# Four equal weight slices, a new order of the first products, one K^T V block and a later place for half of the transposes, in a fused linear-attention and ELU-MLP kernel

## The chip, the cores and the metric

The kernel runs on one core of one Trainium2 chip. Times are device microseconds of that core. "TensorE" (PE) multiplies matrices, PEld is its weight load, "DVE" is VectorE, "ACT" ScalarE, "Pool" GpSimd. PSUM is the memory into which TensorE writes; this kernel divides it into eight banks. The recorded texts call the transposes "turns". A ratio is the mean time of one kernel's runs over that of the other's of the same rounds, so it is not quite the ratio of the medians quoted.

## The reference, cut to what matters

```python
kv  = einsum('bhsd,bhse->bhde', k, v)          # per batch and head: K^T V, 64 x 64
out = einsum('bhsd,bhde->bhse', q, kv)         # "se" below
x   = out / sqrt(mean(out^2) + 1e-6) * g_norm  # RMS norm over each head, 64 wide
h   = x @ w_in                                 # 4608 x 512 @ 512 x 2048
y   = elu(h) @ w_out                           # 4608 x 2048 @ 2048 x 512
```

There are 8 batches, 8 heads and 576 rows a batch. The kernel treats 512 rows of each batch as one group and the 64-row rests of all batches as a ninth.

## The kernel before: the parts that the change touches

The load of `w_in` in five uneven slices (a slice holds columns, and product `f` of the MLP needs columns 128 f to 128 f + 127 over all four chunks `c` of 128 rows). Pool issues these loads; they turn float32 into bfloat16 on the way.

```python
edges = (0, 512, 768, 1280, 1664, 2048)
for lo, hi in zip(edges, edges[1:]):
    load_w_in(slice(lo, hi))
```

Batch 0. `x0[:, c]` is the normalised input's chunk c. It comes out of a chain through TensorE, ACT and DVE, one chunk after the other. `first(fs, cs)` emits the products of those f for those c, c outermost; product f is complete after c = 3.

```python
products = {0: pair[:, 0, :], 1: pair[:, 1, :], 2: bank(6), 3: bank(7), 4: bank(0)}
first((0, 1, 2, 3), (0,))
mean0[3] = bank(2)
mean_first(3); log_first(3); exp_first(3); scale_first(3)      # makes x0[3]
first((0, 1, 2, 3), (1,))
first((4,), (0, 1))
first((0, 1, 2, 3, 4), (2,))
products[5] = bank(1)
first((5,), (0, 1, 2))
first((0, 1, 2, 3, 4, 5), (3,))
# ... then ELU of the pair (0, 1), of (2, 3), of (4, 5)
for i in range(3, 8):                                         # mm1(0, i): products 2i, 2i+1
    mm1(0, i, relu=i in (3, 5, 7), home={5: "m2", 6: "at"}.get(i, "m1"))()
```

`mm1(0, 4)` writes the two banks that the pair had, so it must wait until DVE has read the pair.

Batch 1's attention is woven into batch 0's second matrix product `mm2`:

```python
at["kv0"]()                       # K^T V, half of the heads, with its eviction by ACT
for j in order[:3]:
    mm2(0, j, 8, 10)
at["kv1"]()                       # the other half
mm2(0, order[3], 8, 10)
at["se"](...)
# ... norm, mul0, mul1 (DVE), more mm2, then:
        if j == 0:
            at["x0"]()            # transposes of rows half 0 by TensorE; ACT: PSUM -> xT
at["x1"]()                        # the same for half 1; DVE: PSUM -> xT
# ...
for cs in (slice(0, 256), slice(256, G)):     # batch 1's first products, by column halves
    for f in range(4):
        for c in range(KC):
            nc.tensor.matmul(firsts[f // 2][:, f % 2, cs], lhsT=w_in_sb[:, c, ...], rhs=xT[1](c, cs), ...)
```

`x0` and `x1` put their transposes into the two halves of one PSUM tile, `at`. The first column half needs only `x0`, the second needs `x1`.

## Time and profile before

| | before |
|---|---|
| time, median of 6 runs | 285.84 us (285.73 to 286.19) |
| span of the profiled run | 284.1 us |
| TensorE busy | 275.6 us, 97% |
| start to start of 512-column products | 216 ns (8 in 1.73 us) |

The page of the profile, its line of busy times and its chain of waits:

```profile
PE 275.6 (97%) x2131; PEld 131.0 (46%) x2162; DVE 159.2 (56%) x231; ACT 153.1 (54%) x221; POOL 54.8 (19%) x95
...
PE 88%; ACT 4%; DVE 3%; DMA 2%; issue 1%; another core or an unknown queue 1%; SPq 0%; DVEq 0%
```

TensorE is the limit. The list of waits for TensorE (who waited for whom, microseconds in total, times, longest):

```profile
PE bank L529 <- DVE zeros L506: 1.2, 1, 1.2
PE at L305 <- ACT xT L312: 0.4, 1, 0.4
PE h_ps L398 <- DVE gT L429: 0.3, 1, 0.3
PE bank L607 <- DMA w_in_sb<-in_moe_w_in_dram: 0.3, 1, 0.3
...
```

These idle times understate what is lost. A 512-column product lasts 379 ns in the trace, but the next starts after 216 ns, so a product that starts late first uses up 0.16 us of overlap before the engine counts as idle. The loss is the start-to-start time less 216 ns: an idle of 0.30 is a loss of 0.46. Three losses and two blocks stand in the timeline of TensorE (start, length, what, how many; in brackets the idle time before it and what ended it):

```profile
14.49 0.60 PE L607 MATMUL h_ps<-xT,w_in_sb 128*128 128x512 bf16 x2
...
16.91 0.61 PE L607 MATMUL bank<-xT,w_in_sb 128*128 128x512 bf16 x2 [0.30 <-DMA w_in_sb<-in_moe_w_in_dram]
...
20.37 1.89 PE L398 MATMUL h_ps<-xT,w_in_sb 128*128 128x512 bf16 x8
22.57 3.61 PE L398 MATMUL h_ps<-xT,w_in_sb 128*128 128x512 bf16 x16 [0.31 <-DVE gT L429]
...
33.02 1.08 PE L185 MATMUL at<-ident,q_pk 128*64 128x128 bf16 x32
...
37.59 0.48 PE L174 MATMUL at<-v_pk,k_pk 64*64 64x64 bf16 x36
38.00 1.25 PE L445 MATMUL o_ps<-w_out_sb,gT 128*128 128x512 bf16 x5
39.40 0.48 PE L174 MATMUL at<-v_pk,k_pk 64*64 64x64 bf16 x36
...
40.35 0.41 PE L201 MATMUL at<-kv_sb,qT 64*128 64x64 bf16 x16
...
47.30 0.61 PE L305 MATMUL at<-ident,xs 128*128 128x128 bf16 x8 [0.37 <-ACT xT L312]
47.74 2.46 PE L803 MATMUL h_ps<-xT,w_in_sb 128*128 128x256 bf16 x21
```

To be seen: product 4 waits at 16.91 for its slice of `w_in` (landed 16.86); `mm1(0,4)` waits at 22.57 for DVE to read the pair; K^T V of batch 1 (line 174) comes in two blocks, after the first transpose of q (line 185) and before "se" (line 201); and `x1`'s transposes (line 305) wait at 47.30 for ACT's `xT`, after which the products of line 803 follow at once.

### The profile page before, as it was taken

Reading aid. Unit: us, or ns where it says so; the run is one execution under the profiler, and the core shown is the slowest. Engines: PE = TensorE matmul, PEld = TensorE weight load, DVE = VectorE, ACT = ScalarE, POOL = GpSimd, SP = SyncE. Lnnn points to the kernel's source line nnn. Section 1 sums busy time; section 2 is a strip of 40 time slices with the busy share of each in tenths; the row PEclk is TensorE's granted clock in tenths of the full one; section 3 lists DMA queues with packets and bytes.
Section 4 is the critical chain, followed back from the end, with each engine's and each line's share of the span. In section 5 each row is a group of like instructions: output and inputs, shape, how many; then the busy total and the mean of one; then the engine's idle time right before and its main releaser. Section 6 shows DMA issues by size and latency. Waiting matters only on the chain.

```text
span 284.1 us, 5184 instructions
## 1 busy us (share of the span) xinstructions
PE 275.6 (97%) x2131; PEld 131.0 (46%) x2162; DVE 159.2 (56%) x231; ACT 153.1 (54%) x221; POOL 54.8 (19%) x95
## 2 busy tenths in 40 slices
PE   8999999999999999999999999999999999999994
PEld 3434545545444444444444444444444444444443
DVE  2339516598378636934684458544864486444400
ACT  2769545766496338633773378246923692333311
POOL 7834402261421061004210421012000000000000
PEclk9999999999999999999999999999999999999999
DMA  7999999796994589357934794355253123010122
GB/s 195 204 204 202 206 202 178 219 140 118 199 183 75 150 121 196 74 146 95 221 77 119 110 215 90 96 127 157 45 90 89 77 45 102 2 74 0 74 76 74
DMA packets 56507, 35.99 MB, mean 127 GB/s; under 512 B 32804, under 2 KB 54052, under 8 KB 56484
## 3 DMA queue, kind: packets, MB, share of 16 engines
q0 software_dynamic: 20736, 17.30, 40.1%
q1 hardware_dynamic: 35348, 17.83, 23.7%
q10 hardware_dynamic: 400, 0.52, 0.5%
q8 instruction: 17, 0.28, 0.4%
q14 instruction: 6, 0.05, 0.1%
HBM read 36.70 MB, written 9.44 MB: 162 GB/s over the span
## 4 chain that ended last, share of the span: by engine, by line
PE 88%; ACT 4%; DVE 3%; DMA 2%; issue 1%; another core or an unknown queue 1%; SPq 0%; DVEq 0%
PE h_ps L398 39%; PE o_ps L445 36%; PE o_ps L857 5%; DMA st_q<-in_q_dram 2%; PE at L174 2%; PE h_ps L803 1%; DVE ss L218 1%; PE at L201 1%; ACT elu_e L410 1%; ACT sq L213 1%; PE at L398 1%; PE bank L577 1%; PE bank L529 1%; ACT o_sb L458 1%
## 5 line engine op out<-in xcount | busy, mean ns | idle before, releaser
L398 PE MATMUL h_ps<-xT,w_in_sb 128*128 128x512 bf16 x524 | 123.7, 379 | 0.5 <-DVE gT L429 0.3
L445 PE MATMUL o_ps<-w_out_sb,gT 128*128 128x512 bf16 x488 | 118.1, 379 | 1.3 <-issue 0.2
L410 ACT ACTIVATE elu_e<-h_ps 128x1024 bf16<-128x1024 f32 (+1 forms) x72 | 70.9, 996 | 84.3 <-PE h_ps L398 78.9
L398 PEld LDWEIGHTS <-w_in_sb 128*128 128x128 bf16 x536 | 50.9, 98 | 62.0 <-DVE xT L333 1.7
L445 PEld LDWEIGHTS <-gT 128*128 128x128 bf16 x512 | 49.6, 98 | 58.8
L421 DVE TENSOR_SCALAR elu_e<-elu_e 128x1024 bf16<-128x1024 bf16 (+1 forms) x75 | 32.0, 426 | 73.0 <-ACT elu_e L410 73.0
L429 DVE TENSOR_TENSOR gT<-elu_e,h_ps 128x1024 bf16<-128x1024 bf16 (+1 forms) x53 | 62.6, 1181 | 5.9 <-DVE elu_e L421 0.5
L218 DVE TENSOR_REDUCE ss<-sq 128x16 f32<-128x1024 bf16 x16 | 19.3, 1218 | 13.2 <-ACT sq L213 12.3
L458 ACT COPY o_sb<-o_ps 128x512 f32<-128x512 f32 x32 | 18.5, 586 | 14.4 <-PE o_ps L445 14.4
L150 POOL COPY q_bf<-q_pk 128x512 bf16<-128x512 bf16 x24 | 14.7, 643 | 22.8 <-DMA q_pk<-in_q_dram 22.8
L416 ACT ACTIVATE elu_h<-h_ps 128x1024 bf16<-128x1024 f32 (+1 forms) x19 | 18.5, 989 | 0.0
L429 DVE TENSOR_TENSOR gT<-elu_e,elu_h 128x1024 bf16<-128x1024 bf16 x19 | 13.3, 699 | 2.5 <-ACT elu_h L416 1.2
L857 PE MATMUL o_ps<-w_out_sb,gT 128*128 128x512 bf16 (+1 forms) x79 | 14.0, 336 | 0.1
L125 POOL COPY gate<-qT 1x1 bf16<-1x1 bf16 x6 | 1.1, 180 | 63.9 <-DMA qT<-q_bf 63.9
L229 DVE TENSOR_TENSOR xs<-at,ss 128x512 bf16<-128x512 f32 x18 | 11.5, 682 | 1.2 <-ACT ss L225 1.2
L104 POOL DMA_DIRECT2D q_pk<-in_q_dram x14 | 10.7, 771 | 3.8 <-DMA w_out_sb<-in_moe_w_out_dram 1.7
L857 PEld LDWEIGHTS <-gT 128*128 128x128 bf16 x80 | 7.7, 98 | 6.4 <-DVE gT L429 0.4
L213 ACT ACTIVATE sq<-at 128x1024 bf16<-128x1024 f32 x9 | 9.4, 1044 | 1.6 <-PE at L201 1.6
L118 POOL DMA_DIRECT2D v_pk<-in_v_dram x12 | 8.6, 716 | 3.7 <-DMA w_out_sb<-in_moe_w_out_dram 2.1
L118 POOL DMA_DIRECT2D k_pk<-in_k_dram x12 | 8.3, 694 | 4.7 <-DMA w_in_sb<-in_moe_w_in_dram 3.0
L529 PE MATMUL bank<-zeros 128*128 128x512 bf16 x19 | 7.3, 508 | 1.4 <-DVE zeros L506 1.2
L865 ACT COPY o_last<-o_ps 128x512 f32<-128x512 f32 (+1 forms) x5 | 2.5, 500 | 10.8 <-PE o_ps L857 10.8
(73 smaller groups left out, 140.0 us busy)
## 6 DMA issues: line engine op xcount, KB each, us to landing
out_dram<-o_sb SPq DMA_DIRECT2D x16, 512.0 KB, 3.0
q_pk<-in_q_dram POOLq DMA_DIRECT2D x14, 256.0 KB, 4.9
k_pk<-in_k_dram POOLq DMA_DIRECT2D x6, 576.0 KB, 8.0
v_pk<-in_v_dram POOLq DMA_DIRECT2D x6, 576.0 KB, 11.2
w_out_sb<-in_moe_w_out_dram POOLq DMA_DIRECT2D x3, 512.0 KB, 14.8
st_q<-in_q_dram SPq DMA_DIRECT2D x2, 512.0 KB, 4.9
w_in_sb<-in_moe_w_in_dram POOLq DMA_DIRECT2D x2, 512.0 KB, 8.9
st_q<-in_q_dram SPq DMA_DIRECT2D x16, 64.0 KB, 2.5
```

The lines of the kernel that those rows point to most:

```text
L118: nc.gpsimd.dma_start(out=raw[name, b].rearrange("p h j d -> p h (j d)")[:, hs], in_=in_[:, hs])
L150: eng.tensor_copy(out=out_, in_=in_)
L213: nc.scalar.activation(sq, se_ps, AF.Square)
L218: nc.vector.reduce_sum(out=ss, in_=sq.rearrange("p c (h e) -> p (c h) e", h=H), axis=AX.X)
L398: nc.tensor.matmul(h_ps[a][:, cs], lhsT=w_in_sb[:, c, f * P : f * P + P], rhs=x(c, cs), start=(c == 0), stop=(c == KC - 1),)
L410: nc.scalar.activation(e[:, lo:hi, :], ps, AF.Exp)
L416: nc.scalar.activation(h[:, lo:hi, :], ps, AF.Relu)
L421: nc.vector.tensor_scalar(out=e[:, lo:hi, :], in0=e[:, lo:hi, :], scalar1=1.0, scalar2=1.0, op0=ALU.min, op1=ALU.subtract,)
L429: nc.vector.tensor_tensor(out=gT[T][:, 2 * i + lo : 2 * i + hi, :], in0=e[:, lo:hi, :], in1=h, op=ALU.add if relu else ALU.max,)
L445: nc.tensor.matmul(o_ps[T, j], lhsT=gT[T][:, f, j * P : j * P + P], rhs=w_out_sb[:, f, :], start=(f == 0), stop=(f == FC - 1),)
L458: nc.scalar.copy(o_sb[T][:, j % 2, :], o_ps.pop((T, j)))
L857: nc.tensor.matmul(ps, lhsT=gT[B][:, f, j * P : j * P + P], rhs=w_out_sb[:, f, cols], start=(f == 0), stop=(f == FC - 1),)
```

## The change

Its intent, as far as the edit shows it, is to have the first pair of products ready earlier, so that ACT and DVE start the ELU earlier, at the price of bringing products 4 and 5 later; to load `w_in` in fewer, equal pieces; to save one K^T V block; and to do something useful with the wait before `x1`, whose transposes move to a later place, behind the first half of batch 1's products over the first columns.

```diff
-    edges = (0, 512, 768, 1280, 1664, 2048)
+    edges = (0, 512, 1024, 1536, 2048)
...
-    first((0, 1, 2, 3), (1,))
-    first((4,), (0, 1))
-    first((0, 1, 2, 3, 4), (2,))
     products[5] = bank(1)
-    first((5,), (0, 1, 2))
-    first((0, 1, 2, 3, 4, 5), (3,))
+    first((0, 1, 2, 3), (1, 2))
+    for f in (0, 1, 2, 3):
+        first((f,), (3,))
+    for f in (4, 5):
+        first((f,), (0, 1, 2, 3))
...
-    at["kv0"]()
-    for j in order[:3]:
+    mm2(0, order[0], 8, 10)
+    at["kv"]()
+    for j in order[1:]:
         mm2(0, j, 8, 10)
-    at["kv1"]()
-    mm2(0, order[3], 8, 10)
...
-    at["x1"]()
...
+    head_x1 = at["x1"]
...                                   # in batch 1's first products, after f's c loop:
+            if cs.start == 0 and f == 1:
+                head_x1()
```

## The prediction

> **What bounds the kernel.** TensorE. The page of before has it busy 275.6 us of 284.1 (97%), and the chain of waits is 88% PE. The list of waits shows only about 2.9 us of PE idling named to a cause, 1.2 of it at the start. So nothing here can win much: only the stalls before 52 us can move. A 512-column product starts every 216 ns in the timeline (8 in 1.73 us), which agrees with the Trainium skill, "TensorE: Matmul & The Clock Gate", "Back-to-back issue gap" (N/2.4 + 2.5 ns, isolated). Measured by start-to-start minus 216 ns, the stalls are:
> - 16.91 us: 0.46 us, product 4 waits for the second w_in slice (landed 16.86);
> - 22.57 us: 0.47 us, mm1(0,4) waits for its banks until DVE has read the first pair (22.51);
> - two K^T V blocks in batch 1: 0.50 us each; the single block of batch 2 costs 0.80, so the split costs 0.2;
> - 47.30 us: 0.53 us, x1's turns wait for ACT's xT of x0.
>
> **The change.** PE and DVE keep the same number of instructions; ACT has one eviction fewer, Pool one load and some rows fewer.
>
> 1. Slices. DMA stays saturated to 50 us (about 205 GB/s). Packets of 512 B took 60 ns, of 768 B 79, of 1024 B 98, so equal slices save queue time: I estimate 0.25 us for all loads behind. The second slice is larger and lands about 17.0-17.9 instead of 16.86. By "DMA: Bandwidth & Descriptors", "Why a DMA increments its semaphore by 16 and not by 1", the slowest of 16 engines sets a landing; the trace agrees: a slice's packets end about 1 us before it lands.
>
> 2. Order of first products. Products 0-3 over c=2 follow at once, waiting for x0[2] (DVE ends 16.49): stall 0.1. Over c=3 they need x0[3] (17.91), and no filler is left: a new stall of 0.55 from 17.42 to 17.97. The 0.46 stall goes, as products 4 and 5 come at 18.83, after their slice. They end at about 20.56 (before 20.37), 0.2 later. But the pair is ready at 18.6 instead of 19.7, so ACT and DVE run 1.1 us ahead, DVE is done with the pair at 21.4, and mm1(0,4) starts without a stall at 22.28 instead of 22.57. Net gain 0.28.
>
> 3. One K^T V: gains 0.2. It comes at about 37.7, its second half at 38.1; the last v lands at 37.6-37.8, so a wait there is small or none. Its eviction has 1.3 us of products before se.
>
> 4. x1 inside. The first products themselves need ACT's xT, so the 0.53 stall stays and only changes its name. Then x1 comes 0.87 us later, DVE's xT (0.75 us, starting 0.33 after the last turn) ends at 49.65 on the old clock, and the second column half, ready at 49.49, waits: a loss of 0.2.
>
> All of it is on PE's chain, and after 52 us PE waits for nothing, so the sum passes through: -0.28 -0.20 +0.21 = about -0.27 us.
>
> **Predicted:** 285.5 us, 8 in 10 between 285.0 and 286.0; faster by over 2%: 0.01, within 2%: 0.98, slower by over 2%: 0.01.
>
> **What would show it.** The stall at product 4 and at mm1(0,4) gone; a new wait of about 0.55 us on DVE's xT near 18 us; first exp near 18.6; one K^T V block, se about 0.48 us earlier; a wait of about 0.5 on ACT's xT before the first batch-1 products and about 0.2 on DVE's xT before their second half. The rest shifted, equal in shape.
>
> **What would make it wrong.** The second slice landing after 18.8; v's last half landing after 38.1; x1 not waiting for xT but something I misread, so that the swap frees 0.5 us; DMA delay shifting a later wait onto PE.

## The result

| | before | after |
|---|---|---|
| time, median of 6 runs each | 285.84 us (285.73 to 286.19) | 285.62 us (285.57 to 285.80) |
| ratio, 95% interval | | 0.999 (0.9977 to 1.0003) |
| span of the profiled run | 284.1 us | 283.7 us |
| ACT instructions counted | 221 | 220 |
| Pool instructions counted | 95 | 94 |

The predicted time was 285.5 us, and the measured one lies within its range; so does the time of before, so the range alone tests little. The times alone do not separate the two kernels, since the interval contains 1. The trace does separate them, as the same anchors can be compared in both. First the page's lines, then the waits of TensorE in the kernel after:

```profile
PE 274.4 (97%) x2131; PEld 130.5 (46%) x2162; DVE 159.9 (56%) x231; ACT 153.1 (54%) x220; POOL 53.5 (19%) x94
...
PE 90%; ACT 3%; DVE 3%; DMA 2%; issue 1%; SPq 0%
```

```profile
PE bank L529 <- DVE zeros L506: 1.2, 1, 1.2
...
PE h_ps L607 <- DVE xT L598: 0.4, 1, 0.4
PE h_ps L802 <- ACT xT L312: 0.4, 1, 0.4
...
```

The waits for the slice of `w_in` and for the pair (`L398 <- DVE gT`) are gone. A wait for DVE's `xT` on line 607 is new. The wait for ACT's `xT` is as long as before, 0.4 us, and has only changed its owner: it now stands on the products (line 802) instead of on `x1`'s transposes (line 305). The timeline of TensorE after:

```profile
14.37 0.61 PE L607 MATMUL h_ps<-xT,w_in_sb 128*128 128x512 bf16 x2
...
17.85 0.59 PE L607 MATMUL h_ps<-xT,w_in_sb 128*128 128x512 bf16 x2 [0.43 <-DVE xT L598]
...
20.43 5.34 PE L398 MATMUL h_ps<-xT,w_in_sb 128*128 128x512 bf16 x24
...
32.61 1.08 PE L185 MATMUL at<-ident,q_pk 128*64 128x128 bf16 x32
...
37.62 0.78 PE L174 MATMUL at<-v_pk,k_pk 64*64 64x64 bf16 x72
...
39.73 0.41 PE L201 MATMUL at<-kv_sb,qT 64*128 64x64 bf16 x16
...
46.69 1.03 PE L802 MATMUL h_ps<-xT,w_in_sb 128*128 128x256 bf16 x8 [0.37 <-ACT xT L312]
47.55 0.61 PE L305 MATMUL at<-ident,xs 128*128 128x128 bf16 x8
48.00 2.22 PE L802 MATMUL h_ps<-xT,w_in_sb 128*128 128x256 bf16 x17
```

The 24 products from 20.43 run without a break, so `mm1(0,4)`, the ninth of them, starts at 22.16 by the trace. That is 7.79 us after the first product at 14.37; before it was 22.57 - 14.49 = 8.07.

The next table divides the traces into segments between starts of TensorE instructions. "q" is the first transpose of batch 1's q, "se" the first product of that name, "half" the last of the 32 half-width first products of batch 1.

| segment, us | before | after | difference |
|---|---|---|---|
| start to first product with w_in | 14.49 | 14.37 | -0.12 |
| first product to q (order of first products) | 18.52 | 18.24 | -0.28 |
| q to se of batch 1 (K^T V) | 7.33 | 7.12 | -0.21 |
| se to last half-width product (x1's place) | 10.78 | 10.99 | +0.21 |
| from there to se of batch 2 | 13.10 | 13.10 | 0.00 |
| from there to the last product | 215.80 | 215.81 | +0.01 |

The first line is not credited to the change: it follows when the first slice lands (at 14.45 before and at 14.32 after), and over the 13 traces that start lies between 14.27 and 14.56, the earliest and the latest both with the old slices. The other lines sum to -0.27 us. The prediction said -0.28, -0.20 and +0.21.

### The profile page after: what moved, and what is told of

It reads as the page before. It is cut to its first block, busy times and chain, and to the rows that moved or that the text cites. A ratio compares the mean times of both kernels' runs of the same rounds, so it can differ in the third digit from the quotient of the medians.

```text
span 283.7 us, 5180 instructions
## 1 busy us (share of the span) xinstructions
PE 274.4 (97%) x2131; PEld 130.5 (46%) x2162; DVE 159.9 (56%) x231; ACT 153.1 (54%) x220; POOL 53.5 (19%) x94
## 4 chain that ended last, share of the span: by engine, by line
PE 90%; ACT 3%; DVE 3%; DMA 2%; issue 1%; SPq 0%
PE h_ps L398 39%; PE o_ps L445 36%; PE o_ps L858 5%; DMA st_q<-in_q_dram 2%; PE at L174 2%; PE h_ps L802 1%; DVE ss L218 1%; PE at L201 1%; PE bank L607 1%; ACT sq L213 1%; PE at L398 1%; PE bank L577 1%; PE bank L529 1%; ACT o_sb L458 1%; PE se_ps L201 1%
## 5 line engine op out<-in xcount | busy, mean ns | idle before, releaser
L398 PE MATMUL h_ps<-xT,w_in_sb 128*128 128x512 bf16 x524 | 123.6, 380 | 0.2
L398 PEld LDWEIGHTS <-w_in_sb 128*128 128x128 bf16 x536 | 50.8, 98 | 61.5 <-DVE xT L333 1.7
L529 PE MATMUL bank<-zeros 128*128 128x512 bf16 x19 | 6.6, 465 | 1.4 <-DVE zeros L506 1.2
## 6 DMA issues: line engine op xcount, KB each, us to landing
w_out_sb<-in_moe_w_out_dram POOLq DMA_DIRECT2D x3, 512.0 KB, 15.5
```

What stands on the lines that cost most here:

```text
L398: nc.tensor.matmul(h_ps[a][:, cs], lhsT=w_in_sb[:, c, f * P : f * P + P], rhs=x(c, cs), start=(c == 0), stop=(c == KC - 1),)
```

## The experiments

The first four runs do one part of the change alone on the kernel before. All kernels gave correct results. Median times: 287.14 (e1_slices), 285.59 (e2_order), 285.77 (e3_kv), 286.27 (e4_x1), with before at 285.87 in the same rounds.

| segment, us | before | e1 slices | e2 order | e3 kv | e4 x1 | e5 x1 back | e6 filler | e7 own tile | e8 all |
|---|---|---|---|---|---|---|---|---|---|
| first product to q | 18.52 | 19.63 | 18.24 | 18.66 | 18.39 | 18.24 | 17.60 | 18.54 | 17.68 |
| q to se | 7.33 | 7.33 | 7.33 | 7.12 | 7.33 | 7.11 | 7.33 | 7.33 | 7.17 |
| se to last half-width product | 10.78 | 10.78 | 10.78 | 10.78 | 10.98 | 10.78 | 10.78 | 10.39 | 10.38 |
| to se of batch 2 | 13.10 | 13.40 | 13.15 | 13.10 | 13.30 | 13.19 | 13.10 | 13.24 | 13.11 |
| to the last product | 215.80 | 215.80 | 215.80 | 215.94 | 215.80 | 215.79 | 215.80 | 215.80 | 216.42 |

### The four slices alone (e1_slices)

```diff
-    edges = (0, 512, 768, 1280, 1664, 2048)
+    edges = (0, 512, 1024, 1536, 2048)
```

> Before with the four equal w_in slices alone. Mine (stall sum): the second slice lands at about 17.9 us instead of 16.86, so product 4, which before's order puts fifth, waits for it from about 16.45; that stall grows from 0.46 to about 1.45 us, mm1(0,4)'s stall of 0.47 stays since the pair is also 1 us later, and the kernel is SLOWER by 0.8 to 1.1 us (about 286.8). Rival D (the gain of the change is the saved queue time of equal slices): faster by 0.2 us. Rival X (the gain is x1 inside): no difference.

Measured: 287.14 us, ratio 1.0048 (1.0036 to 1.0061), so slower by about 1.3 us. The timeline of TensorE in this kernel:

```profile
17.84 0.60 PE L607 MATMUL bank<-xT,w_in_sb 128*128 128x512 bf16 x2 [1.40 <-DMA w_in_sb<-in_moe_w_in_dram]
...
23.50 3.61 PE L398 MATMUL h_ps<-xT,w_in_sb 128*128 128x512 bf16 x16 [0.31 <-DVE gT L429]
```

The second slice landed at 17.79, and product 4 waited 1.40 us idle for it (1.56 lost). The wait for the pair stayed. The segment grew by 1.11 us, the size expected. The rest of the loss, 0.3 us, came in the fourth segment, on the way to se of batch 2, and was not expected; it is taken up below. The rival that the slices make the gain falls: alone they cost more than four times what the whole change gains.

### The order alone (e2_order)

```diff
-    first((0, 1, 2, 3), (1,))
-    first((4,), (0, 1))
-    first((0, 1, 2, 3, 4), (2,))
     products[5] = bank(1)
-    first((5,), (0, 1, 2))
-    first((0, 1, 2, 3, 4, 5), (3,))
+    first((0, 1, 2, 3), (1, 2))
+    for f in (0, 1, 2, 3):
+        first((f,), (3,))
+    for f in (4, 5):
+        first((f,), (0, 1, 2, 3))
```

> Before with the new order of the first products alone, old uneven slices. Mine: products 4 and 5 come at 18.8, after the old second slice too, so the order gains all of its 0.28 us without the slices: mm1(0,4) starts 7.79 us after the first product instead of 8.07, new wait of about 0.55 us on x0[3] near 17.9; time 0.2 to 0.35 us under before. Rival D: 0, or a loss of 0.1. Rival X: a loss of 0.2 (the new wait on x0[3] is bigger than the old one on the slice).

Measured: 285.59 us, ratio 0.9991 (0.9978 to 1.0003); the medians differ by 0.28 us, but the interval contains 1, so here too the trace has to decide. First product to q took 18.24 us, exactly as in the full change. So the slices add nothing once the order is new, and they are harmless only because of it: products 4 and 5 come at 18.7 us, after both the old second slice (16.70) and the new one (17.89).

### One K^T V block alone (e3_kv)

```diff
-    at["kv0"]()
-    for j in order[:3]:
+    mm2(0, order[0], 8, 10)
+    at["kv"]()
+    for j in order[1:]:
         mm2(0, j, 8, 10)
-    at["kv1"]()
-    mm2(0, order[3], 8, 10)
```

> Before with the one K^T V block in batch 1 alone. Mine: 0.20 us faster; se starts 0.20 us earlier after mm1(0,4) (17.57 instead of 17.78 us after it), the block costs 0.80 instead of 2 x 0.50 us, no wait for v (landing 37.8, second half needed at 38.4). Rivals D and X: no difference.

Measured: 285.77 us, ratio 1.0 (0.9987 to 1.0012). The times are inconclusive. In the trace q to se is 7.12 instead of 7.33 us, the 0.21 us expected. In this execution other things took it back: the second slice landed at 17.06, so the wait at product 4 cost 0.59 instead of 0.46 us, and a wait of 0.16 us idle for DVE stood at 92 us (a DVE operation of 0.69 us had taken 1.14 at 79.20 us; see e8_all). The part is shown by the trace, not by the times.

### x1 inside alone (e4_x1)

```diff
-    at["x1"]()
...
+    head_x1 = at["x1"]
...
+            if cs.start == 0 and f == 1:
+                head_x1()
```

> Before with x1's turns inside batch 1's first products alone. Mine: SLOWER by 0.20 us: the 0.5 us wait for ACT's xT of x0 stays and stands before the first batch-1 product instead of before x1, and the second column half waits 0.2 us for DVE's xT of x1. Rival X: faster by 0.3 to 0.5 us, since the turns fill the wait. Rival D: no difference.

Measured: 286.27 us, ratio 1.0015 (1.0001 to 1.0028): slower, by the medians 0.40 us. The timeline of TensorE:

```profile
45.79 1.03 PE L445 MATMUL o_ps<-w_out_sb,gT 128*128 128x512 bf16 x4
47.18 1.03 PE L803 MATMUL h_ps<-xT,w_in_sb 128*128 128x256 bf16 x8 [0.37 <-ACT xT L312]
48.05 0.61 PE L305 MATMUL at<-ident,xs 128*128 128x128 bf16 x8
48.50 2.98 PE L803 MATMUL h_ps<-xT,w_in_sb 128*128 128x256 bf16 x24
```

The wait for ACT's `xT`, 0.37 us idle, is the same as before and stands before the products. The segment is 0.20 us longer, as expected: the second column half starts 0.31 us after its predecessor instead of 0.11, released by DVE's `xT`. Another 0.20 us was lost in the next segment. The rival that this part frees the wait falls.

### The change without that part (e5_x1_back)

```diff
(against the changed kernel)
+    at["x1"]()
...
-    head_x1 = at["x1"]
...
-            if cs.start == 0 and f == 1:
-                head_x1()
```

> The changed kernel with x1's turns back in front of batch 1's products. Mine: 0.2 us faster than the changed kernel, so about 0.48 us under before. Rival X (x1 inside is the gain): slower than the changed kernel, at or above before.

Measured: 285.38 us, ratio to before 0.9979 (0.9966 to 0.9991), before at 285.94 in these rounds (also for the next three runs). The segment of `x1` is back at 10.78 us. This is the first faster version whose interval excludes 1. The changed kernel was timed in other rounds, so that it is 0.2 us slower is read from the segments.

### Filling the new wait (e6_filler)

The new order leaves TensorE idle before c = 3, because nothing else is emitted that could run. With the old, smaller second slice (landed 16.7), product 4 can run there.

```diff
(against before)
-    first((0, 1, 2, 3), (1,))
-    first((4,), (0, 1))
-    first((0, 1, 2, 3, 4), (2,))
     products[5] = bank(1)
-    first((5,), (0, 1, 2))
-    first((0, 1, 2, 3, 4, 5), (3,))
+    first((0, 1, 2, 3), (1, 2))
+    first((4,), (0, 1, 2))
+    first((0, 1, 2, 3, 4), (3,))
+    first((5,), (0, 1, 2, 3))
```

> Before's uneven slices with an order that fills the wait for x0[3]: products 0-3 over c=0,1,2, then product 4 over c=0,1,2 (its small slice landed at 16.86, needed at 17.4), then products 0-4 over c=3, then product 5. Mine: no stall but 0.1 us before c=2; mm1(0,4) starts about 7.25 us after the first product instead of 8.07; 0.84 us faster than before (about 284.95). Rival N (some other limit in batch 0, such as ACT or DVE, hands the gain back before 60 us): mm1(0,4) early but a new stall of the same size later, total gain under 0.4 us.

Measured: 284.93 us, ratio 0.997 (0.9957 to 0.9982). The timeline of TensorE:

```profile
16.31 0.59 PE L607 MATMUL h_ps<-xT,w_in_sb 128*128 128x512 bf16 x2
16.74 1.24 PE L607 MATMUL bank<-xT,w_in_sb 128*128 128x512 bf16 x5
17.83 0.59 PE L607 MATMUL h_ps<-xT,w_in_sb 128*128 128x512 bf16 x2
18.26 1.67 PE L607 MATMUL bank<-xT,w_in_sb 128*128 128x512 bf16 x6
19.77 5.34 PE L398 MATMUL h_ps<-xT,w_in_sb 128*128 128x512 bf16 x24
```

No line has an idle time. First product to q took 17.60 us, 0.92 less than before, and no later segment gave anything back. The uneven slices that the change took away are what makes this possible: the equal second slice landed at 17.89 in the changed kernel, too late to fill a wait that ends at 17.85. That is read from the landing; this order was not run with the equal slices.

### x1 in a tile of its own (e7_x1_own)

```diff
(against before)
-    at["x1"]()
+    at["x1"](ps_m1.tile([P, 2, G], FP32, name="xt_ps", tag="mm1")[:, 0, :])
```

> Before with x1's turns in a PSUM tile of their own instead of the second half of x0's tile. Mine: x1 no longer waits for ACT's xT but runs during it; the first batch-1 product still waits for ACT's xT, about 0.1 us instead of 0.53; 0.35 to 0.44 us faster. Rival W (x1 waits for the normalised rows from DVE, not for the shared tile): the wait stays, no difference.

Measured: 285.36 us, ratio 0.998 (0.9967 to 0.9994). The timeline of TensorE:

```profile
45.81 1.03 PE L445 MATMUL o_ps<-w_out_sb,gT 128*128 128x512 bf16 x4
46.68 0.61 PE L305 MATMUL xt_ps<-ident,xs 128*128 128x128 bf16 x8
47.21 3.70 PE L803 MATMUL h_ps<-xT,w_in_sb 128*128 128x256 bf16 x32
```

The transposes no longer wait: they run while ACT reads the other tile. The wait was one for the shared tile, although `x0` and `x1` use different halves of it, and not for DVE's rows. The segment is 0.39 us shorter, as expected; 0.14 us were lost in the next one, to a DVE operation that took 0.59 instead of 0.42 us (see e8_all). So these two segments account for only 0.25 of the 0.58 us by which the medians differ. In the traced run 0.10 us more came from an earlier landing of the first slice, and the end of the run, from the last product, was 0.2 us shorter (3.90 instead of 4.10 us), here and in every kernel below that has this edit. The traces place this in the program's closing steps, after the last output has landed: DVE's last closing instruction (DRAIN) starts 0.09 us after the semaphore instruction before it, in before 0.45 us. Why is not shown.

### All of it together (e8_all)

It is e6_filler and e7_x1_own, and one K^T V block placed after half of the `mm2` pieces, so that it comes after the last landing of v:

```diff
(against e6_filler with e7_x1_own's edit)
-    at["kv0"]()
-    for j in order[:3]:
+    for j in order[:2]:
         mm2(0, j, 8, 10)
-    at["kv1"]()
-    mm2(0, order[3], 8, 10)
+    at["kv"]()
+    for j in order[2:]:
+        mm2(0, j, 8, 10)
```

> All that pays: before's slices with the filler order, one K^T V placed two products pairs later (after half of the products over chunk 8-9, since it now comes earlier than v's last landing), x1 in its own tile. Mine: -0.84 -0.20 -0.35 = 1.3 to 1.45 us faster than before (about 284.4 to 284.5), less up to 0.2 us where the last w_out load (landed at 41.6) or v's (37.8) is waited for. Rival N: gain under 0.8 us.

Measured: 284.83 us, ratio 0.9961 (0.9948 to 0.9973), so about 1.1 us faster, 0.2 to 0.35 us less than expected. The first three segments gave about what they should (-0.84, -0.16 and -0.40 us). The last in the table, from se of batch 2 on, is 0.62 us longer. The waits of TensorE name DVE, and the timelines of DVE and Pool show why:

```profile
PE h_ps L398 <- DVE gT L429: 0.5, 1, 0.5
```

```profile
82.16 0.91 DVE L429 TENSOR_TENSOR gT<-elu_e,elu_h 128x1024 bf16<-128x1024 bf16 x1
82.99 0.83 DVE L421 TENSOR_SCALAR elu_e<-elu_e 128x1024 bf16<-128x1024 bf16 x1
```

```profile
81.81 2.49 POOL L150 COPY q_bf<-q_pk 128x512 bf16<-128x512 bf16 x3 [2.58 <-DMA q_pk<-in_q_dram]
```

For comparison the same two DVE operations in the kernel before:

```profile
83.70 0.69 DVE L429 TENSOR_TENSOR gT<-elu_e,elu_h 128x1024 bf16<-128x1024 bf16 x1
84.31 0.42 DVE L421 TENSOR_SCALAR elu_e<-elu_e 128x1024 bf16<-128x1024 bf16 x1
```

Beside Pool's three copies of batch 4's q, DVE's operations took 0.91 and 0.83 us instead of 0.69 and 0.42, together 0.63 us more. From there DVE hands the delay on to TensorE at 91 us. Pool's copies start when q lands, at a time set by DMA; DVE's operations come at a time set by TensorE. Here DVE's pair came 1.54 us earlier than in before, and the copies 1.42 us later (81.81 instead of 80.39, as q landed later), and so they met. The Trainium skill, "SBUF — State Buffer", "Who interferes with whom", says that the two engines share one pair of ports, that a `tensor_scalar` in one of DVE's two-port modes contends for it, that a `tensor_tensor` with both inputs in SBUF contends with GpSimd's reads, and that `tensor_reduce` never contends on this chip. The traces agree, though they do not show DVE's mode: the two forms stretched here are the bf16 `tensor_scalar` and the `tensor_tensor` with both inputs in SBUF (`gT<-elu_e,elu_h`), while the form that reads PSUM (`gT<-elu_e,h_ps`) stayed at 1.22 us, and the reductions at 1.21 where copies ran beside them (e3_kv at 80.26, e11_all_gate_k at 84.49).

Counted over all 13 traces, operations of `elu_e<-elu_e` (512 and 1,024 elements) and `gT<-elu_e,elu_h` took over 20 ns more than usual 111 times, each time beside an operation or a DMA issue of Pool; the 937 that ran beside none were all of usual length, and 174 ran beside Pool unharmed. Most stretches cost nothing: before has eight of 60 ns or more and none shows among TensorE's waits, and in e8_all an operation at 50.09 us took 0.93 instead of 0.43 us while its segment stayed at 13.11. Time is lost only where TensorE soon waits for the result, as at 91 us.

The small losses of the earlier runs are of the same kind. In e1_slices a DVE operation of the form that otherwise takes 0.29 us took 0.63 beside Pool's issue of the q and k loads (0.34 more, for 0.3 lost); in e4_x1 one of 0.42 took 0.67 beside the issue of the k and v loads (0.25 more, for 0.20 lost).

### Two tests of the meeting (e9_filler_own, e10_all_gate)

e9_filler_own is e6_filler with e7_x1_own's edit and K^T V as before. e10_all_gate is e8_all with this, which holds back three of the four copies of batch 4:

```diff
-            if j == J - 1:
+            if j == (0 if b == 4 else J - 1):
                 after(bf["v", b][0:1, 0, 0, 0:1])
```

> The filler order and x1's own tile, K^T V left as before. The combined kernel of the last call reached 60 us 1.5 us ahead of before but lost about 0.6 us at 85 to 91 us, where TensorE waited for DVE, whose bf16 ops had run at 0.8 to 0.9 us instead of 0.4 to 0.7 beside Pool's copies of q of batch 4. Theory C (that loss is a chance meeting of Pool's copies, timed by DMA, with DVE's ops, timed by TensorE): this one is 1.2 to 1.35 us ahead at 60 us; if the meeting is missed the whole of it reaches the end, about 284.6; if it happens, the loss stands beside DVE ops over 0.5 us in the trace. Rival L (a lead of over 1.1 us is always handed back, because ACT and DVE have no slack there): se of batch 2 early, but loss of 0.2 us or more at 85 to 91 us with every DVE op at its usual length.

> The combined kernel, with Pool's first three copies of q of batch 4 held back until v of batch 4 has landed (about 86 to 89 us) instead of starting at q's landing (about 82 us). Theory C: DVE's ops at 82 to 85 us are back at 0.42 and 0.69 us, the waits of TensorE for DVE at 85 and 91 us shrink to under 0.2 us in all unless the copies now meet other DVE ops just as badly, and the kernel is 0.3 to 0.6 us faster than the combined one (284.3 to 284.5). Rival L: the waits stay at 0.6 us, no difference.

Measured: e9_filler_own 285.15 us (ratio 0.9977), e10_all_gate 284.92 us (ratio 0.9962, runs from 284.17 to 285.44), with before at 285.92. e9 lost 0.63 us at 91 us with a lead of only 1.20 us; two DVE operations of 0.42 us took 0.85 and 0.61 (at 82 and 88 us), 0.62 us too much together. In e10 the operations at 82 to 85 us were back at their lengths, but the copies now ran from 87.61 us and met those at 88: 0.91 instead of 0.69 and 0.83 instead of 0.42, again 0.63 us. So as a repair e10 failed, but the meeting moved with the copies, and three times the loss equals the excess of the DVE operations that Pool's copies ran beside. "A lead over 1.1 us is always handed back, whatever meets" would need losses with DVE at its usual lengths, and there was none. What is true of it is that DVE has no slack there: each stretch at 82 to 89 us was paid in full. That the transfers themselves and not Pool stretch DVE does not fit e10: k and v of batch 4 were on their way at 82 to 84 us there too (they landed at 84.24 and 87.37), and DVE kept its lengths.

### Copies between, beside other DVE work (e11_all_gate_k)

```diff
(against e8_all)
+            if b == 4 and j == 0:
+                after(bf["k", b][0:1, 0, 0, 0:1])
             if j == J - 1:
```

> The combined kernel, with Pool's first three copies of q of batch 4 held back until k of batch 4 has landed (84.2 and 85.6 us in the last two traces), so that they run beside DVE's head sums and its scaling out of PSUM (about 84.4 to 87.5 us) instead of beside its bf16 elementwise ops. Theory C: no DVE elementwise op over its usual length at 80 to 91 us, the 0.63 us loss there gone, a lead of about 1.5 us kept to the end: 284.2 to 284.4. Rival L (no slack for a lead over 1.1 us, whoever meets whom): a loss of 0.4 us or more there with every DVE op at its usual length, 284.8.

Measured: 284.24 us, ratio 0.9948 (0.9934 to 0.9961): the fastest of all, 1.6 us under before by the medians. Its five runs fall into two groups, 284.22, 284.23 and 284.24, and 284.73 and 284.77. The profiled run is the 284.77, and shows a meeting, though another one. Pool and then DVE in that trace:

```profile
84.99 1.70 POOL L152 COPY q_bf<-q_pk 128x512 bf16<-128x512 bf16 x3
88.10 0.69 POOL L125 COPY gate<-v_pk 1x1 bf16<-1x1 bf16 x1 [1.40 <-DMA v_pk<-in_v_dram]
88.73 0.60 POOL L152 COPY q_bf<-q_pk 128x512 bf16<-128x512 bf16 x1
```

```profile
82.22 0.69 DVE L431 TENSOR_TENSOR gT<-elu_e,elu_h 128x1024 bf16<-128x1024 bf16 x1
82.83 0.42 DVE L423 TENSOR_SCALAR elu_e<-elu_e 128x1024 bf16<-128x1024 bf16 x1
...
88.66 0.95 DVE L423 TENSOR_SCALAR elu_e<-elu_e 128x1024 bf16<-128x1024 bf16 x1
```

The three copies moved (1.70 us for the three) now meet nothing, and DVE's operations at 82 us are at 0.69 and 0.42. The fourth copy and its gate met the one at 88.66: 0.95 instead of 0.42, and 0.53 us were lost at 91 us. That is also the distance between the two groups of runs. It is argued, not shown, that the three fast runs are those without this meeting, as only one run was traced.

## Why the prediction was right

- **TensorE bounds, so only its stalls before 52 us count.** Right. From there to the last product both traces take the same time within 0.01 us. It holds for this change: the larger leads of e8_all to e11_all_gate_k made a new wait at 91 us.
- **Order of the first products, -0.28 us.** Right, and alone (e2_order) as in the whole. The new wait before c = 3 was to lose 0.55 us and lost 0.59 (idle 0.43 plus 0.16); that before c = 2 lost 0.07 instead of 0.1.
- **One K^T V block, -0.20 us.** Right: 0.21 to 0.22 us in three traces (after, e3_kv, e5_x1_back).
- **x1 inside, +0.21 us.** Right: +0.21 and +0.20 us. The wait for ACT's `xT` only changed its name, and e7_x1_own shows what would have removed it.
- **Equal slices save 0.25 us of queue time.** Wrong: nothing was saved. The landing of the last `w_in` slice was 8.62 us after that of the first before and 8.61 after. The term was estimated from packet times (60 ns at 512 B against 98 ns at 1,024 B). It did not matter, because none of the later loads was waited for.
- **The second slice lands at 17.0 to 17.9 us, in time.** Right: 17.89, needed at 18.7. By the Trainium skill, "DMA: Bandwidth & Descriptors", "Why a DMA increments its semaphore by 16 and not by 1", a load counts as landed when the slowest of 16 engines has posted. The trace of before fits but does not show it: 14 of the 512 packets of the second slice started after 15.5 us, the last ended at 16.32, and the slice landed at 16.86; which engine moved a packet is not in the trace.
- **Not in the prediction:** the first product started 0.12 us earlier in the profiled run, with the landing of the first slice, which no part of the argument foresaw and which was luck; and DVE operations can be stretched by Pool. Neither decided this result, but the second cost 0.14 to 0.65 us in several experiments.

What stays open is why 0.2 us are saved at the end of the kernels with the own tile, and which runs of a kernel meet Pool's copies where, as each kernel was traced once.

## What to carry to other kernels

On an engine that is 97% busy, add up start-to-start times at its few stalls and ask of each edit which stall it removes, which it creates, and which it merely renames: here a moved block waited for the same ACT instruction under another line number. Test the parts of a bundle alone, since two of the four (the slices and the moved transposes) were losses or useless, and the small slice that was given up was what could fill the new wait. Then look for what a lead will collide with: here the work timed by DMA did not move with TensorE, and 0.6 of a 1.5 us lead was lost where Pool's copies met DVE's operations.

## What the Trainium skill lacked or had wrong

- "TensorE: Matmul & The Clock Gate", "Back-to-back issue gap", gives about 131 ns a product as the sustained rate at 512 columns and calls 216 ns the isolated gap. In this kernel 216 ns is the sustained gap: it is the median over 981 pairs of successive products in before's trace, each with its own weight load, at a granted clock of 0.998.
- "SBUF — State Buffer", "Who interferes with whom", says that DVE and GpSimd block each other fully on their shared ports, but gives no sizes for the small operations of a kernel. Here DVE's 1,024-element bf16 `tensor_scalar` went from 0.42 to as much as 0.95 us, its `tensor_tensor` with both inputs in SBUF from 0.69 to as much as 1.14, and Pool's copies from 0.6 to as much as 1.13 (e1_slices at 80.47). DVE was also slowed while Pool merely issued loads (0.29 to 0.63, 0.42 to 0.67); for such issues the page names only the case that DVE holds them up, though its general rule, that whoever issues first blocks the other, would cover the reverse.
- "DMA: Bandwidth & Descriptors", "Specifications", puts line rate at 512 B and more. Here, in loads that turn float32 into bfloat16, packets of 512 B took 60 ns and of 1,024 B 98 ns, so 8.5 against 10.4 B a nanosecond; that section gives no times of packets. It is not contradicted: the queue moved 198 to 207 GB/s from 12 to 26 us whatever the mix of sizes, and equal slices of 1,024 B packets did not land sooner.
- No page that I found has the cost of breaking a run of wide products by a block of 64 x 64 ones: two blocks of 36 cost 0.50 us each, one of 72 cost 0.80. It would belong to "TensorEngine Tiling (Array Packing)", which has no figure for it.
